# Gate and up as seven stacked half products from the fifth chunk on, with weight forms prepared in chunks 1 to 3

## Chip, core and metric

The kernel runs on one core of a Trainium2 chip. The metric is the device time of one execution in microseconds. The core has TensorE (PE, with weight loads shown apart as PEld), VectorE (DVE), ScalarE (ACT), GpSimd (POOL) and SyncE (SP), whose queue issues all DMA transfers here.

## What is computed

The reference normalises 8192 tokens of 448 channels, mixes them with a spectral block (a Fourier transform along the tokens, a two-layer block-diagonal network on the frequencies, the inverse transform), and then applies a gated feed-forward layer. All six modulation rows come from a small vector c.

```python
h = _layernorm(x) * (1 + ca) + sa
x = x + ga * _A_ref(h, A_w1, A_b1, A_w2, A_b2)      # rfft2, block MLP, irfft2
h = _layernorm(x) * (1 + cb) + sb
x = x + gb * ((_gelu(h @ w_gate) * (h @ w_up)) @ w_down)   # 448 -> 1792 -> 448
```

The change is in the last line's two first products, gate and up.

## The kernel before

Two stages follow each other. The spectral stage (up to about 383 us of the trace) works through frequency groups, in a list of steps; `at(i, ...)` puts side jobs into step i, among them the loading and splitting of the gate and up weights (`load_w`, `weights_hi`, `weights_lo`, lines 692 and 787 to 795, in steps 17 to 31). The feed-forward stage is a loop of 32 chunks `i` of 256 tokens (`CB` = 2 blocks of 128), and in it 14 ticks `k` (line 1272). Feature tile f of 128 is written as f = t + 7q, tile t from 0 to 6, half q 0 or 1, and k = 2t + q.

Every f16 product is done in a high and a low part: a value is scaled, its f16 rounding is the high part, the remainder the low part, and high x high, high x low and low x high are summed in PSUM. `gate_up` (line 1096) issues for a tick 20 matmuls of 256 columns (line 1087): gate and up, each with three full tiles of 128 of the 448 channels in three variants plus one half tile of 64 channels that carries two variants at once. The remaining low half tiles (64 rows) are issued for a pair of tiles together, two at a time on different halves of the array (lines 1112 to 1116). That makes 308 matmuls a chunk. `gate_up_out` (line 1120) takes gelu of the gate on ACT (1123), multiplies by up on DVE (1128) and forms four sums of the 2 x 2 blocks (two halves q, two token blocks) on POOL (1134 to 1137), in place in an eight-part tile x. `quantize` (1139) splits seven of the parts into f16 high on ACT (1145) and low on DVE (1146).

`down` (line 1158) multiplies them with seven weight forms (Strassen's scheme in Winograd's form: seven products of halves instead of eight): 7 products of 7 tiles of 3 matmuls with 224 columns (1153 to 1155), 147 a chunk. It runs for chunk i - 1 at tick k = 2 of chunk i, in one piece. ACT and DVE read the products, POOL finishes the rows (1190, 1167, 1168), and SP stores them (1197).

The same loop prepares chunk i + 2 at fixed ticks (`hooks`, line 1201): load of v, g and the tokens, `split_g` and `split_v` at k = 3 (high on ACT, low on POOL, line 107), `inverse` at k = 6 (987 to 989, six matmuls of 448 columns), `residual` (998, 999), statistics, `norm2` (1036, 1037), `pack_hi` and `pack_lo` at k = 13 (1042, 1049 to 1051), and at k = 0 of the next chunk four DMA transposes into `nt` (1057). The order of instructions on each engine is the order of the program text; an engine that waits holds up all that stands behind it. PSUM has eight banks: `pa` and `pb` for gate and up, `pc` and `pd` for the rest, two of each.

Of the kernel before, what the change touches and what calls it, by code (L numbers as in the profile page):

```python
# [10 lines left out]
F32 = mybir.dt.float32  # L11
# [26 lines left out]
NTT = len(PKO)  # L38
LAM = 0.01
# [6 lines left out]
def spectral_geglu(ctx, tc, x, w1, b1, w2, b2, wg, wu, wd, cvec, wmod, cf1, cs2, cmi, cgm, out):  # L46
# [10 lines left out]
    sd = dram.tile([NP, 128, 4, HC], F32, name="sd")  # L57

    cpool = ctx.enter_context(tc.tile_pool(name="cpool", bufs=1))
    psum = ctx.enter_context(tc.tile_pool(name="psum", bufs=2, space=bass.MemoryType.PSUM))  # L60
# [18 lines left out]
    sw = cpool.tile([128, 2], F32, name="sw")  # L79
    dg = cpool.tile([128, 1], F32, name="dg")  # L80
# [238 lines left out]
    with ExitStack() as bctx:  # L319
# [359 lines left out]
        def row_scales():  # L679

            GL.tensor_scalar(cb_r, cb_r, 1.0, None, op0=ALU.add)
            tiny.extend([free] * 2)
            for j, r in enumerate((cb_r, sb_r)):
                VL.tensor_reduce(rmax[:, j : j + 1], r, mybir.AxisListType.X, ALU.max, apply_absolute_value=True)
            bnd = cpool.tile([128, 1], F32, name="hb")
            VL.scalar_tensor_tensor(bnd, rmax[:, 0:1], 21.2, rmax[:, 1:2], op0=ALU.mult, op1=ALU.add)
            VL.tensor_scalar(bnd, bnd, 1.01, 1e-30, op0=ALU.mult, op1=ALU.add)
            pow2(sk, bnd)
            GL.tensor_scalar(sb_r, sb_r, sk, None, op0=ALU.mult)
            GL.tensor_scalar(cb_r, cb_r, sk, None, op0=ALU.mult)  # L690
# [48 lines left out]
        def scales1():  # L739

            ni = nrm.bitcast(I32)
            VL.tensor_scalar(ni, ni, 1, 0x7F800000, op0=ALU.logical_shift_right, op1=ALU.bitwise_and)
            VL.tensor_scalar(ni, ni, float(65 << 23), None, op0=ALU.add)
            mx = mpool.tile([128, 2], F32, name="mx")
            VL.tensor_reduce(mx, nrm, mybir.AxisListType.X, ALU.max)

            hb2 = mpool.tile([128, 1], F32, name="hb2")
            mx2 = mpool.tile([128, NFT], F32, name="mx2")
            first = [
                lambda: G.tensor_tensor(hb2, rmax[:, 0:1], rmax[:, 1:2], ALU.add),  # L750
                lambda: G.tensor_tensor(hb2, hb2, hb2, ALU.mult),
                lambda: G.tensor_scalar(hb2, hb2, 1.02 * D, 1e-30, op0=ALU.mult, op1=ALU.add),
            ]

            then = [
                lambda: G.tensor_tensor(mx2, nrm[:, 0], nrm[:, 1], ALU.mult),
                lambda: G.tensor_scalar(mx2, mx2, hb2, None, op0=ALU.mult),
            ]
            all_sum(mxa, mx, 2, first, then)
            pow2(sw, mxa)  # L760
            VL.tensor_tensor(sa_act, mx2[:, :NP], mx2[:, NP:], ALU.max)
# [24 lines left out]

        def weights_hi(pr, j):
            raw = raws[("w", pr, j)]
            fs = slice(pr * F + j * 256, pr * F + (j + 1) * 256)
            S.activation(wh[:, :, fs], raw, AF.Copy, scale=sw[:, pr : pr + 1])  # L790

        def weights_lo(pr, j):
            raw = raws.pop(("w", pr, j))
            fs = slice(pr * F + j * 256, pr * F + (j + 1) * 256)
            V.scalar_tensor_tensor(wl[:, :, fs], raw, sw[:, pr : pr + 1], wh[:, :, fs], op0=ALU.mult, op1=ALU.subtract)

# [52 lines left out]
        wpool = ctx.enter_context(tc.tile_pool(name="wpool", bufs=1))  # L852
        wh = wpool.tile([128, 4, 2 * F], F16, name="wh")
        wl = wpool.tile([128, 4, 2 * F], F16, name="wl")

# [3 lines left out]

        def x1_tile(i):  # L860

            pool, n = (cp, 2) if i % 3 else (ep, 1)
            return pool.tile([128, CB, D], F32, tag="x1", name="x1", bufs=n)
# [63 lines left out]

        fctx = ExitStack()
# [4 lines left out]
        for j in range(14):  # L933
            at(17 + j, "load", pre, fp, ("w", j % 2, j // 2), load_w, j % 2, j // 2)
            at(18 + j, "act", weights_hi, j % 2, j // 2)
            at(18 + j, "dve", weights_lo, j % 2, j // 2)
# [12 lines left out]
    with ExitStack() as cctx:  # L949
        cp = cctx.enter_context(tc.tile_pool(name="cp", bufs=1, side="right"))  # L950
        H = 128 * CB
        wds = wds + [cp.tile([128, 2, 7, HC], F16, name=f"wd{t}") for t in range(len(wds), NP)]
        nts, acts, pgu = {}, {}, {}

# [13 lines left out]
        def split_v(i, cs=slice(0, D)):  # L968
            n = nxt[i]
            if "vh" not in n:  # L970
                n["vh"] = cp.tile([128, CB, D], F32R, tag="vh", name="vh")
                n["vl"] = cp.tile([128, CB, D], F32R, tag="vl", name="vl")
            for b in each(i):
                split(n["vh"][:, b, cs], n["vl"][:, b, cs], n["v"][:, b, cs], el=G)
# [64 lines left out]
        def pack_hi(i):  # L1039
            pk = cp.tile([128, CB, PKW], F16, tag="pk", name="pk")  # L1040
            for b in each(i):
                S.copy(pk[:, b, 0:D], nxt[i]["n"][:, b])
            nxt[i]["pk"] = pk

        def pack_lo(i):
            n, pk = nxt[i]["n"], nxt[i]["pk"]
            for b in each(i):
                e = V if i == 0 else G
                e.tensor_tensor(pk[:, b, 448:512], n[:, b, 384:448], pk[:, b, 384:448], ALU.subtract)
                e.tensor_copy(pk[:, b, 512:576], pk[:, b, 384:448])  # L1050
                e.tensor_tensor(pk[:, b, 576:960], n[:, b, 0:384], pk[:, b, 0:384], ALU.subtract)
            nts[i] = cp.tile([128, NTT, H], F16, tag="nt", name="nt", bufs=2)

# [30 lines left out]
        def gu(i, t, q, pr, w, rows, tw, tn, start, stop):  # L1084

            f0 = pr * F + (t + NP * q) * 128
            T.matmul(  # L1087
                pgu[i, t, q][:, pr * H : (pr + 1) * H],
                w[rows, tw, f0 : f0 + 128],
# [6 lines left out]
        def gate_up(i, k):  # L1096
# [7 lines left out]
            seq = [(wh, j, j) for j in range(4)] + [(wh, j, j + 5) for j in range(3)] + [(wl, j, j) for j in range(3)]  # L1104
# [5 lines left out]
            elif q == 1:  # L1110

                for pr in range(2):
                    for u in range(2):
                        for qq in range(2):
                            it = divmod(i * NP + t + u, NP)
                            gu(*it, qq, pr, wl, halfs[qq], 3, 3 + qq, u == 1 and pr == 0, u == 0)
# [3 lines left out]
        def gate_up_out(i, t, q):  # L1120
# [6 lines left out]
            dst = x[:, 1:3] if q else x[:, 0::7]  # L1127
# [3 lines left out]
            if q:  # L1131
                e = V if (i, t) == (nch - 1, NP - 1) else G
                a11, a12, a22, s1, s2, s3, s4, a21 = (x[:, j] for j in range(8))
                e.tensor_tensor(s1, a21, a22, ALU.add)  # L1134
                e.tensor_tensor(s2, s1, a11, ALU.subtract)  # L1135
                e.tensor_tensor(s3, a11, a21, ALU.subtract)  # L1136
                e.tensor_tensor(s4, a12, s2, ALU.subtract)  # L1137
# [11 lines left out]
        def product(i, ps, ka, kb, ts=range(NP)):  # L1149
            ps = ps[:, :HC]  # L1150
            for t in ts:
                ac = acts[(i, t)]
                T.matmul(ps, ac[:, 0, ka], wds[t][:, 0, kb], start=t == 0, stop=False)  # L1153
                T.matmul(ps, ac[:, 0, ka], wds[t][:, 1, kb], start=False, stop=False)  # L1154
                T.matmul(ps, ac[:, 1, ka], wds[t][:, 0, kb], start=False, stop=t == NP - 1)  # L1155
            return ps

        def down(i):
            p1, p4, u2, u4 = (cp2.tile([128, HC], F32, tag=n, name=n) for n in ("p1", "p4", "u2", "u4"))
            o = cp2.tile([128, CB, D], F32, tag="o", name="o")  # L1160
# [11 lines left out]
            b1, b2 = bank("pd", "pdn"), bank("pc", "pdn")  # L1172

            product(i, b1, 0, 0, range(NP - 1))
            product(i, b2, 1, 1, range(NP - 1))
            S.copy(p1, product(i, b1, 0, 0, [NP - 1]))
            V.tensor_tensor(o11, product(i, b2, 1, 1, [NP - 1]), p1, ALU.add)
            if last:
                finish(0, 0, G)
            for fn, *args in second["down"] if i == 0 else []:  # L1180
                fn(2, *args)
            S.copy(p4, product(i, bank("pd", "pdn"), 2, 5))
            V.tensor_tensor(u2, product(i, bank("pd", "pdn"), 4, 6), p1, ALU.add)
            V.tensor_tensor(u4, product(i, bank("pd", "pdn"), 3, 3), u2, ALU.add)
            for fn, *args in second["down2"] if i == 0 else []:
                fn(2, *args)
            p7 = product(i, bank("pd", "pdn"), 5, 4)
# [3 lines left out]
            p3 = product(i, bank("pd", "pdn"), 6, 2)  # L1191
# [8 lines left out]

        hooks = {
            0: [(1, transposes_dma)],
# [8 lines left out]
            13: [(2, pack_hi), (2, pack_lo)],  # L1211
# [44 lines left out]
        cp2 = cctx.enter_context(tc.tile_pool(name="cp2", bufs=1))  # L1256
# [15 lines left out]
        for i in range(nch):  # L1272
            for k in range(NFT):
# [3 lines left out]
                if k % 2 == 1 and i + k > 1 and (i, k) != (nch - 1, NFT - 1):  # L1277
                    quantize(*((i, k // 2 - 1) if k > 1 else (i - 1, NP - 1)))
                if (i, k) == (nch - 1, NFT - 2):
                    quantize(i, NP - 2)  # L1280
# [3 lines left out]
                if k == 2 and i > 0:  # L1284
                    down(i - 1)
                    if i == 1:
                        transposes_dma(2, range(1, 2))
                for fn, *args in first.pop(i * NFT + k, []):
# [7 lines left out]
        quantize(nch - 1, NP - 1, (0, 3, 7))  # L1296
        down(nch - 1)
# [75 lines left out]
```

## Time and profile before

| what | value |
|---|---|
| median of 3 runs | 1938.26 us (1938.06 to 1939.17) |
| the profiled execution | 1940.48 us, its span 1938.7 us |
| granted TensorE clock, mean | 0.994 |
| instructions | 43005 |
| DMA moved | 163.79 MB, mean 84 GB/s |

A page or view of the profile covers the one profiled execution. An engine's busy time is the time in which one of its instructions was executing; a matmul's time is modelled from start to drain, so matmuls that follow at 109 ns are each shown with 273 ns. In a group's row stand line, engine, operation, tiles written and read, shape and count, then busy time in us, mean ns of one, then idle time of the engine before them and who ended it. In a windows row stand the window, its length, the busy time (and count) of each engine, the granted clock, the DMA share and GB/s.

### The profile page before, as it was taken

Reading aid. Unit: us, or ns where it says so; the run is one execution under the profiler, and the core shown is the slowest. Engines: PE = TensorE matmul, PEld = TensorE weight load, DVE = VectorE, ACT = ScalarE, POOL = GpSimd, SP = SyncE. Lnnn points to the kernel's source line nnn. Section 1 sums busy time; section 2 is a strip of 40 time slices with the busy share of each in tenths; the row PEclk is TensorE's granted clock in tenths of the full one; section 3 lists DMA queues with packets and bytes.
Section 4 is the critical chain, followed back from the end, with each engine's and each line's share of the span. In section 5 each row is a group of like instructions: output and inputs, shape, how many; then the busy total and the mean of one; then the engine's idle time right before and its main releaser. Section 6 shows DMA issues by size and latency. Waiting matters only on the chain.

```text
span 1938.7 us, 43005 instructions
## 1 busy us (share of the span) xinstructions
PE 1903.1 (98%) x17620; PEld 1694.9 (87%) x17620; DVE 1109.8 (57%) x2352; ACT 788.3 (41%) x1338; POOL 1159.4 (60%) x1466
## 2 busy tenths in 40 slices
PE   7899999899999999999999999999999999999999
PEld 3599999778888888888888888888888888888898
DVE  8677788786555555555555555555555555555533
ACT  5677888553333333333333333333333333333322
POOL 3157655256666666666666666666666666666644
PEclk9899999999999999999999999999999999999999
DMA  9999777641111111111111112111111111111000
GB/s 346 314 286 257 203 188 197 171 140 49 45 43 45 43 41 45 45 41 46 41 46 43 42 44 44 43 43 44 43 44 43 43 43 43 43 43 43 21 11 20
DMA packets 157981, 163.79 MB, mean 84 GB/s; under 512 B 77908, under 2 KB 136152, under 8 KB 157784
## 3 DMA queue, kind: packets, MB, share of 16 engines
q1 hardware_dynamic: 157784, 161.05, 28.7%
q8 instruction: 138, 2.26, 0.5%
q14 instruction: 59, 0.48, 0.1%
HBM read 97.44 MB, written 47.25 MB: 75 GB/s over the span
## 4 chain that ended last, share of the span: by engine, by line
PE 86%; DVE 4%; issue 3%; ACT 3%; DMA 2%; POOL 2%; SPq 1%; ACTq 0%; POOLq 0%; DVEq 0%
PE pgu L1087 53%; PE pdn L1155 8%; PE pdn L1154 8%; PE pdn L1153 8%; PE ps L202 2%; DVE y L463 2%; PE pi L989 1%; PE pi L988 1%; PE pi L987 1%; POOL yl L107 1%; DMA raw<-in_B_w_up 1%; DVE st L163 0%; ACT th L105 0%; PE ps L368 0%; PE ps L370 0%
## 5 line engine op out<-in xcount | busy, mean ns | idle before, releaser
L1087 PE MATMUL pgu<-nt,wh 128*128 128x256 f16 x6272 | 834.3, 273 | 2.7 <-DVE x L1128 2.6
L1087 PEld LDWEIGHTS <-wh 128*128 128x128 f16 x6272 | 602.7, 98 | 101.5 <-issue 33.9
L1123 ACT ACTIVATE gel<-pgu,dg 128x256 f32<-128x256 f32 x448 | 200.3, 473 | 792.3 <-PE pgu L1087 756.2
L1087 PE MATMUL pgu<-nt,wl 128*128 128x256 f16 (+1 forms) x3584 | 501.3, 272 | 0.4 <-DVE x L1128 0.4
L1155 PE MATMUL pdn<-wd,ac 128*128 128x224 f16 x1568 | 406.1, 259 | 0.2 <-DVE ac L1146 0.2
L1153 PE MATMUL pdn<-wd,ac 128*128 128x224 f16 x1568 | 406.1, 259 | 0.0
L1154 PE MATMUL pdn<-wd,ac 128*128 128x224 f16 x1568 | 406.1, 259 | 0.0
L1134 POOL TENSOR_TENSOR x<-x 128x128 f32<-128x128 f32 x223 | 239.9, 1076 | 260.3 <-DVE x L1128 228.1
L1146 DVE SCALAR_TENSOR_TENSOR ac<-x,sa_act,ac 128x896 f16<-128x896 f32 (+1 forms) x225 | 308.9, 1373 | 83.3 <-ACT ac L1145 83.3
L1087 PEld LDWEIGHTS <-wl 128*128 128x128 f16 (+1 forms) x3584 | 297.9, 97 | 57.5 <-issue 24.3
L1128 DVE TENSOR_TENSOR x<-pgu,gel 128x256 f32<-128x256 f32 x448 | 179.6, 418 | 276.2 <-ACT gel L1123 275.6
L1145 ACT ACTIVATE ac<-x,sa_act 128x896 f16<-128x896 f32 (+1 forms) x225 | 232.9, 1035 | 49.0 <-POOL x L1137 47.0
L1190 POOL TENSOR_TENSOR o<-u,p 128x224 f32<-128x224 f32 x32 | 21.0, 657 | 291.8 <-DVE u L1189 291.8
L1135 POOL TENSOR_TENSOR x<-x 128x128 f32<-128x128 f32 x223 | 157.5, 706 | 17.5
L1155 PEld LDWEIGHTS <-ac 128*128 128x128 f16 x1568 | 153.4, 98 | 0.5 <-DVE ac L1146 0.5
L1154 PEld LDWEIGHTS <-ac 128*128 128x128 f16 x1568 | 153.4, 98 | 0.4
L1153 PEld LDWEIGHTS <-ac 128*128 128x128 f16 x1568 | 153.4, 98 | 0.4
L107 POOL TENSOR_TENSOR yl<-y,yh 128x448 fp32r<-128x448 f32 x63 | 78.9, 1252 | 75.6 <-ACT yh L105 64.4
L463 DVE SCALAR_TENSOR_TENSOR y<-pm,t 64x224 f32<-64x224 f32 x256 | 99.5, 389 | 41.3 <-ACT t L455 37.4
L1136 POOL TENSOR_TENSOR x<-x 128x128 f32<-128x128 f32 x223 | 113.7, 510 | 0.0
L1137 POOL TENSOR_TENSOR x<-x 128x128 f32<-128x128 f32 x223 | 110.7, 497 | 0.0
L107 POOL TENSOR_TENSOR tl<-tr,th 128x896 f16<-128x896 f32 x30 | 57.3, 1909 | 68.3 <-DMA td<-xt 36.8
(281 smaller groups left out, 2727.7 us busy)
## 6 DMA issues: line engine op xcount, KB each, us to landing
tr<-td SPq DMA_DIRECT2D x64, 224.0 KB, 4.2
vd<-us SPq DMA_DIRECT2D x64, 224.0 KB, 3.5
xx<-in_A_x SPq DMA_DIRECT2D x32, 448.0 KB, 3.2
v<-vd SPq DMA_DIRECT2D x63, 224.0 KB, 2.9
out<-x SPq DMA_DIRECT2D x31, 448.0 KB, 2.7
xt<-in_A_x SPq DMA_DIRECT2D x15, 896.0 KB, 15.3
td<-xt SPq DMA_DIRECT2D x48, 224.0 KB, 4.4
s<-cs SPq DMA_DIRECT2D x20, 256.0 KB, 4.5
```

What stands on the lines that cost most here:

```text
L107: (el or V).tensor_tensor(lo, src, h, ALU.subtract)
L463: V.scalar_tensor_tensor(y[ri * 64 : ri * 64 + 64, gi], pv[si, ri], LAM, tv[si, ri], op0=ALU.add, op1=ALU.min)
L1087: T.matmul(pgu[i, t, q][:, pr * H : (pr + 1) * H], w[rows, tw, f0 : f0 + 128], nts[i][rows, tn, :], start=start, stop=stop, skip_group_che ...
L1123: S.activation(gl, ps[:, :H], AF.Gelu_apprx_tanh, scale=dg)
L1128: V.tensor_tensor(dst, ps[:, H : 2 * H].rearrange("p (b c) -> p b c", b=2), gl.rearrange("p (b c) -> p b c", b=2), ALU.mult)
L1134: e.tensor_tensor(s1, a21, a22, ALU.add)
L1135: e.tensor_tensor(s2, s1, a11, ALU.subtract)
L1145: S.activation(ac[:, 0, k], x[:, k], AF.Copy, scale=sc)
L1146: V.scalar_tensor_tensor(ac[:, 1, k], x[:, k], sc, ac[:, 0, k], op0=ALU.mult, op1=ALU.subtract)
L1153: T.matmul(ps, ac[:, 0, ka], wds[t][:, 0, kb], start=t == 0, stop=False)
L1154: T.matmul(ps, ac[:, 0, ka], wds[t][:, 1, kb], start=False, stop=False)
L1155: T.matmul(ps, ac[:, 1, ka], wds[t][:, 0, kb], start=False, stop=t == NP - 1)
```

## The change

Chunks 0 to 3 (`NSTD` = 4) keep the plain scheme. From chunk 4 on gate and up are computed with seven products as `down` already is: the halves are the two halves q of the features, the two token blocks, and the two halves of 192 channels; the last 64 channels are stacked beside the halves so that tiles of 128 rows are full. One (chunk, tile) is a "period" u = 7i + t. Its matmuls have 128 columns, alternate between gate and up (two banks of one of three PSUM sets), and come in stages a, b, c, d. Partial results are copied inside PSUM (`seed`), out of it (`copy_b`) and joined (`joins`), so a period's work is spread over four: stage_a of u, stage_d of u - 2, stage_c of u - 1, stage_b of u. `down` of chunk i - 1 and the new `winverse` of chunk i + 2 run after the period of tile 2 (`phase`).

The weights' seven forms are made during chunks 1 to 3 (`prep`): loaded, summed on POOL, split on ACT and DVE, and stored to DRAM (`wk`). SBUF holds four slots, each for the forms of one tile; up to chunk 3 the plain weights lie in them. Tiles are visited forward and backward in turn, so that three slots a chunk are loaded again from `wk` (`load_part`, in two parts). The token forms are made on DVE (`token_sums`), ACT (`wpack_hi`) and POOL (`wpack_lo`), and five DMA transposes bring 25 tiles into `nt` (before four bring 8 tiles of 256 columns). The low part of v now lies in v itself. The weights of the spectral stage are loaded by six DMA starts each where it was three, and the scale factor uses another power of two. The core of the diff:

```diff
+NSTD = 4
+WPARTS = ((0, 4), (4, 7))
+    wk = [[dram.tile([128, 2, 2, 2, b - a, 128], F16, name=f"wk{t}{a}") for a, b in WPARTS] for t in range(NP)]
...
+        def load_w2(pool, pr, j):
+            raw = raw_tile(pool).rearrange("p k c -> p (k c)").rearrange("p (e k f) -> p e k f", e=2, k=4)
+            for e in range(2):
+                wsrc = (wg, wu)[pr][:, (2 * j + e) * 128 : (2 * j + e + 1) * 128]
+                dma(raw[:, e, 0:3], wsrc[0:384].rearrange("(t p) f -> p t f", p=128))
+                for rows in rows2:
+                    dma(raw[rows, e, 3], wsrc[384:448])
+            return raw
...
         def weights_hi(pr, j):
-            S.activation(wh[:, :, fs], raw, AF.Copy, scale=sw[:, pr : pr + 1])
+            for w, r in weight_cuts(pr, j):
+                S.activation(w[:, :, 0], r, AF.Copy, scale=sw[:, pr : pr + 1])
...
+        wslot = [wpool.tile([128, 2, 2, 14, 128], F16, name=f"wk{n}") for n in range(4)]
...
-        def down(i):
+        def down(i, banks, mid=lambda n: None):
...
+        def load_part(u, part):
+            a, b = WPARTS[part]
+            dst = wslot[slot_of[u]].rearrange("p r l (g f) x -> p (r l g) f x", g=2)
+            dma(dst[:, :, a:b], wk[torder[u]][part].rearrange("p r l g f x -> p (r l g) f x"))
+        def after(u, part):
+            if u in refill:
+                pending.append((refill[u], part))
...
+        def wpack_lo(i, ks, e=G):
+            for k in ks:
+                for src, hi, los in pieces(i, k):
+                    for a, b, lo in los:
+                        e.tensor_tensor(lo, src[..., a:b], hi[..., a:b], ALU.subtract)
+        def wtransposes(i, gs, w=5):
+            for g in gs:
+                nc.sync.dma_start(
+                    nts[i][:, w * g : w * g + w, :], pkt[:, 128 * w * g : 128 * w * (g + 1)], transpose=True
+                )
...
+        def mm(u, reg, f, x, start=False):
+            ps2, slot, nt = sets[u % 3], wslot[slot_of[u]], nts[u // NP]
+            if f in (A11, S1, S2):
+                terms = [(0, f, x), (0, f, x + 2), (1, f, x), (0, 7 + f, x + 1), (1, 7 + f, x + 1)]
+            else:
+                terms = [(l, f + 7 * g, x + g + 2 * m) for g in range(2) for l, m in ((0, 0), (0, 1), (1, 0))]
+            for j, (hl, wt, xt) in enumerate(terms):
+                for pr in range(2):
+                    T.matmul(
+                        ps2[:, pr, reg * 128 : reg * 128 + 128],
+                        slot[:, pr, hl, wt, :],
+                        nt[:, xt, :],
...
+        def stage_a(u):
+            mm(u, RY, A11, B11, start=True)
+            mm(u, RV, S1, T1)
+            mm(u, RX, A12, B21)
+        def stage_b(u):
+            mm(u, RY, S2, T2)
+        def stage_c(u):
+            mm(u, RV, S3, T3)
+            mm(u, RY, S4, B22)
+        def stage_d(u):
+            mm(u, RV, A22, T4)
+        def copy_b(u):
+            S.copy(sbs[u], sets[u % 3][:, :, 0:256])
+        def seed(u):
+            S.copy(p[:, :, 0:128], p[:, :, 128:256])
+        def joins(u):
+            V.tensor_tensor(c[:, :, 1:3, :], p[:, :, 0:256]..., b[:, :, 0:128]..., ALU.add)
+            V.tensor_tensor(c[:, :, 0, :], p[:, :, 256:384], b[:, :, 128:256], ALU.add)
...
+        def period(u):
+            on(u, stage_a)
+            on(u - 1, seed)
+            for fn, *args in held:
+                fn(*args)
+            held.clear()
+            on(u - 2, joins)
+            on(u - 2, gel3)
+            on(u - 4, quant_lo)
+            on(u - 2, mult3)
+            on(u, copy_b)
+            on(u - 2, stage_d)
+            on(u - 2, lambda v: after(v, 1))
+            on(u - 2, gel1)
+            on(u - 2, mult1)
+            on(u - 2, lambda v: sums(xs[v], G))
+            on(u - 3, quant_hi)
+            on(u - 1, stage_c)
+            on(u, stage_b)
+            on(u, lambda v: after(v, 0))
...
+        def phase(i):
+            pf = sets[(u + 1) % 3]
+            on(u - 3, quant_lo)
+            if j < nch:
+                winverse(j, pf)
+                residual(j)
+            down(i - 1, down_banks(pf), mid)
+        extra = {
+            1: [(2, split_v), (2, split_g), (1, wtransposes, [0])],
+            2: [(1, wtransposes, range(1, 5))],
+            3: [(2, token_sums, 0), (2, wpack_hi, [0, 1]), (2, wpack_lo, [0, 1])],
+            4: [(2, token_sums, 1), (2, wpack_hi, [2]), (2, wpack_lo, [2])],
+            5: [(2, wpack_hi, [3]), (2, wpack_lo, [3]), (3, load_g)],
+            6: [(2, wpack_hi, [4]), (2, wpack_lo, [4]), (3, load_v)],
+        }
...
+                (0, load_forms),
+                (1, form_sums, 0),
+                (1, forms_hi, 0),
+                (2, forms_lo, 0),
+                (2, forms_hi, 1),
+                (2, forms_lo, 1),
+                (3, form_sums, 1),
+                (3, store_forms, 0),
+                (4, forms_hi, 2),
+                (4, forms_hi, 3),
+                (4, forms_lo, 2),
+                (5, forms_lo, 3),
+                (5, store_forms, 1),
+            ):
+                prep.setdefault(NFT + 6 * n + s, []).append((fn, n, *args))
...
+        for u in range(U0, NT_ + 1):
+            period(u)
+            flush()
+            if k == LA:
+                phase(i)
```

`gel3`, `mult3` and the first three quarters of a tile's result (384 columns) come before stage_d, `gel1` and `mult1` (128 columns) after it; `quant_hi` and `quant_lo` do what `quantize` did. `flush` issues the pending loads of weight forms.

## Prediction before the run

> **What bounds the kernel now.** I read the page first, then the busy time by stage, then the groups by line and shape, and last the timeline of single matmuls.
>
> ```profile
> PE 1903.1 (98%) x17620; PEld 1694.9 (87%) x17620; DVE 1109.8 (57%) x2352; ACT 788.3 (41%) x1338; POOL 1159.4 (60%) x1466
> ...
> PE   7899999899999999999999999999999999999999
> ```
>
> TensorE (PE) is busy in every slice and the other engines are not. The next view holds two chunks, all instructions first and then those of L1087 (gate and up) alone:
>
> ```profile
> 812.96:909.44 96.48, 96.48 (x925) 86.34 (x923) 50.33 (x101) 31.42 (x53) 62.25 (x81) 1.00 0.17 44
> ```
>
> ```profile
> 812.96:909.44 96.48, 66.35 (x619) 56.22 (x617) 1.00 0.17 44
> ```
>
> PE has no idle time there at full clock. The code gives 308 gate and up matmuls a chunk, and 2 x 308 = 616 is the 619 of the row with its edges, so a chunk takes 48.24 us. How that divides, from the timeline of PE:
>
> ```profile
> 814.78 0.93 PE L1087 MATMUL pgu<-nt,wh 128*128 128x256 f16 x7
> 815.55 0.49 PE L1087 MATMUL pgu<-nt,wl 128*128 128x256 f16 x3
> 815.88 0.93 PE L1087 MATMUL pgu<-nt,wh 128*128 128x256 f16 x7
> ...
> 819.15 0.26 PE L1153 MATMUL pdn<-wd,ac 128*128 128x224 f16 x1
> ...
> 821.93 0.26 PE L1155 MATMUL pdn<-wd,ac 128*128 128x224 f16 x1
> ...
> 842.54 0.45 PE L987 MATMUL pi<-vh,gh 128*128 128x448 f32 x1
> ...
> 843.66 0.36 PE L989 MATMUL pi<-vl,gh 128*128 128x448 f32 x1
> ```
>
> Ten matmuls of 256 columns start in 815.88 - 814.78 = 1.10 us, 109 ns each. The down matmuls (30 rows from 819.15 to 821.93, 29 steps) come every 96 ns, so the 147 of a chunk take 14.1 us. The six inverse matmuls take 1.3 us. Gate and up keep 48.24 - 14.1 - 1.3 = **32.8 us a chunk**. Anything that gains must shorten that.
>
> **The change part by part. TensorE in chunks 4 to 31.** For one feature tile pair (a "period" of the new loop) stage_a issues 10 + 10 + 12 matmuls, stage_b 10, stage_c 24, stage_d 12: 78 of 128 columns, 546 a chunk, each with a weight load of its own. Columns fall from 308 x 256, less the 14 pairs of half matmuls that run side by side, to 546 x 128, but weight loads rise from 308 to 546. So everything hangs on how fast a load and a 128-column matmul follow each other. The trace has this shape in the spectral stage and in chunk 0:
>
> ```profile
> 117.49 0.22 PE L369 MATMUL ps<-s,th 128*112 128x128 f16 x1
> ...
> 118.72 0.22 PE L370 MATMUL ps<-s,tl 128*112 128x128 f16 x1
> ```
>
> ```profile
> 383.24 0.61 PE L1069 MATMUL ptr<-ident,pk 128*128 128x128 f16 x8
> ```
>
> Of the first stretch these are the first and the last of 23 rows, 22 steps in 1.23 us: 55.9 ns. The eight with full 128x128 weights end 0.61 us after the first began; less one duration of 0.22, seven steps, 55.7 ns. I take 55.9: 546 x 55.9 = 30.5 us, **2.3 us a chunk less, 28 chunks: -64 us**.
>
> The Trainium skill ("TensorE: Matmul & The Clock Gate", section "Back-to-back issue gap") speaks against this: in a stream of load and matmul pairs it gives about 81 ns at 128 columns, which would make an estimated 44.2 us a chunk and the kernel some 320 us slower. This trace disagrees, in short runs only (55.9 ns over 23); a run of 78 is not in it, so the rule stays as the pace of a rival below.
>
> **The other engines inside a period of 78 x 55.9 = 4.36 us.** Times of one instruction, chunks 7 to 15:
>
> ```profile
> L1145 ACT ACTIVATE ac<-x,sa_act 128x896 f16<-128x896 f32 x59 | 61.3, 1038 | 11.7 <-POOL x L1137 11.6
> L1123 ACT ACTIVATE gel<-pgu,dg 128x256 f32<-128x256 f32 x118 | 52.8, 473 | 210.9 <-PE pgu L1087 201.1 <-DVE rcy L118 6.8 <-DVE x L1128 3.0
> ...
> L1176 ACT COPY p<-pdn 128x224 f32<-128x224 f32 x8 | 2.8, 346 | 29.1 <-PE pdn L1155 29.1
> ```
>
> ```profile
> L1146 DVE SCALAR_TENSOR_TENSOR ac<-x,sa_act,ac 128x896 f16<-128x896 f32 x59 | 82.0, 1389 | 20.7 <-ACT ac L1145 20.7
> L1128 DVE TENSOR_TENSOR x<-pgu,gel 128x256 f32<-128x256 f32 x118 | 47.2, 417 | 73.1 <-ACT gel L1123 72.9
> ```
>
> ```profile
> L1134 POOL TENSOR_TENSOR x<-x 128x128 f32<-128x128 f32 x59 | 65.9, 1117 | 59.1 <-DVE x L1128 59.1
> L1135 POOL TENSOR_TENSOR x<-x 128x128 f32<-128x128 f32 x58 | 39.7, 684 | 4.5
> L1136 POOL TENSOR_TENSOR x<-x 128x128 f32<-128x128 f32 x58 | 29.4, 507 | 0.0
> L1137 POOL TENSOR_TENSOR x<-x 128x128 f32<-128x128 f32 x58 | 27.9, 480 | 0.0
> L999 POOL TENSOR_TENSOR x<-x,xx 128x448 f32<-128x448 f32 x18 | 20.0, 1131 | 0.0
> L107 POOL TENSOR_TENSOR vl<-v,vh 128x896 fp32r<-128x896 f32 x9 | 18.8, 2092 | 0.0
> ...
> L1051 POOL TENSOR_TENSOR pk<-n,pk 128x768 f16<-128x768 f32 x8 | 13.2, 1646 | 0.0
> L107 POOL TENSOR_TENSOR gl<-g,gh 128x256 fp32r<-128x256 f32 x8 | 5.8, 722 | 0.0
> ```
>
> ACT: 224 columns cost 346 ns and 896 cost 1038, so about 1.03 ns a column above 0.12. seed (256 columns) 0.38, copy_b (512) 0.65, the two gelus (384 and 128, with L1123's 0.09 more) 0.6 and 0.35, quant_hi 1.04, a piece of wpack_hi 0.3 to 0.8: 3.3 to 3.8 us. DVE: joins (512 and 256 columns) 0.7 + 0.42, quant_lo 1.39, mult3 0.55, mult1 0.3: 3.4. POOL: the four sums 1.12 + 0.68 + 0.51 + 0.48 = 2.79, and wpack_lo's 1600 columns at 1646/768 = 2.1 ns with their overheads, 4.4 us a chunk in four periods: 2.8 to 4.2. All fit, and their waits are covered: b waits for copy_b behind 2.0 us of d and c, c waits for seed behind 2.5 us of a and d, d waits for the joins behind a's 1.8. I charge these **nothing**; the cover ends if an engine needs more than 4.36 us (first rival).
>
> One wait is not covered. split_v and split_g stand on POOL behind the sums of k=1, in the last period before the new winverse. In k=1 stage_d ends 2.45 us in, gel1 at 3.1 and mult1 at 3.5, or at 3.8 where ACT or DVE runs late; the sums end 2.79 later, 1.9 to 2.3 us into k=2, and 2.09 + 0.72 more end at 4.75 to 5.1. Winverse's second matmul wants gl at 4.36 + 0.2. I take the middle, **0.4 us a chunk, +11 us**. Bounds are 0 (POOL's spans are rough and it may be ahead of this) and 2.0 us (the wait and a late refill together). In down nothing else is late: its last tile's quant_lo ends some 1.5 us after the period, and 36 products lie ahead of it, 3.4 us.
>
> **Weight refills.** Three slots a chunk, 5.5 MB, are new on SP's queue. There they stand behind the out store, which waits for POOL's finish (four operations of 1.13, till 4.4 us after down), and four transposes:
>
> ```profile
> 867.02 6.40 SPq L1057 DMA_TRANSPOSE nt<-pk  x4
> ```
>
> ```profile
> xx<-in_A_x SPq DMA_DIRECT2D x32, 448.0 KB, 3.2
> ```
>
> The transposes hold SP for 6.4 us or, with five tiles for four, 8. The second half of the second refill (0.79 MB; 3.2 us by the xx row, twice that at worst) is issued near 11 to 12.5 and lands at 14 to 19 us. stage_c wants it 3 x 4.36 + 2.45 = 15.5 us after down. I take it as just in time: 0.
>
> **Chunks 0 to 3 keep their matmuls,** but chunks 1 to 3 also make the forms.
>
> ```profile
> 425.40:571.20 145.80, 145.80 (x1384) 129.99 (x1382) 82.72 (x174) 47.07 (x80) 93.15 (x118) 1.00 0.18 50
> ```
>
> The columns after the length are PE, loads, DVE, ACT, POOL. Each of seven tiles adds on POOL four sums of 384 columns (0.97 each by L999) and a copy, some 4.9 us. ACT and DVE add 1792 columns, twice their 896-column rows with ten starts: about 3.3 and 3.6. POOL goes to 93.2 + 34 = 127 of 145.8, DVE to 108, ACT to 70. Outside down a chunk has 34 us of PE and POOL would have 31 + 11.5 = 42.6 us of work, so it is 8.4 late when the last tile's sums stand in its queue. The down product needs that tile 10.4 us after its gelu, and its own chain (2.8 + 1.04 + 1.39) takes 5.2: 3.2 us late a chunk, **+10 us** in three chunks. Bounds: 0 and, if ACT also waits for each form load, 25.
>
> **The rest.** The switch at chunk 4 empties the pipeline: the last gelu and product (0.9) and the first copy_b (0.9) are uncovered, and at the end the last tile has its chain of joins, gelus, sums and quant (some 7 us by the times above) behind 63 down matmuls (6.0), an estimated 1 us uncovered: **+3 us**, between 1 and 6. The 14 weight loads of the spectral stage become 84 starts instead of 42, and some ACT and DVE instructions split in two; PE's nines in slices 4 to 8 hide that: 0, at most 3 without that cover.
>
> Sum: -64 + 11 + 10 + 3 = **-40 us**. The profiled execution took 1940.48 us for a span of 1938.7, the median is 1938.26; that span with the 1.8 us around it is 2.2 above the median. I subtract from the median: **1898 us**.
>
> **The rivals.**
>
> *POOL becomes the bound (slower).* A POOL operation that meets a long DVE operation on SBUF is stretched:
>
> ```profile
> 1865.40 1.36 POOL L1135 TENSOR_TENSOR x<-x 128x128 f32<-128x128 f32 x1
> 1866.39 0.42 DVE L1128 TENSOR_TENSOR x<-pgu,gel 128x256 f32<-128x256 f32 x1
> 1866.72 0.45 POOL L1136 TENSOR_TENSOR x<-x 128x128 f32<-128x128 f32 x1
> ```
>
> That is 0.9 us. A tile now has two such DVE operations (quant_lo and mult3) where it had one. Sums with two stretched operations take 4 x 0.45 + 2 x 0.9 = 3.6 us, with wpack_lo's piece 4.7; in four or five periods a chunk PE then waits 0.35 to 0.45, 1.8 us a chunk: 1898 + 50 = **1948**. It decides from 40/28/7 = 0.20 us a period upward. Against it: POOL can pay back in down's 14 us. 11%.
>
> *Refills late.* With landings between 15.5 and 19 us, in the middle 17.2, stage_c waits 1.7 us a chunk: 1898 + 48 = **1946**. For it: the queue is in order and the margin small. Against: the transfers average only 44 GB/s now (last column of the windows). 6%.
>
> *The loads set the pace:* the matmuls do not do what their columns say.
>
> ```profile
> L1087 PEld LDWEIGHTS <-wh 128*128 128x128 f16 x6272 | 602.7, 98 | 101.5 <-issue 33.9
> ```
>
> A load lasts 98 ns. If in a long run loads followed one another, 546 x 98 = 53.5 us, 20.7 more than now: **about 2520**. It decides from 32.8/546 = 60 ns. Against it stand the 55.9 ns, at which loads must overlap. By the skill's 81 ns it would be an estimated 2260. 4%.
>
> *Forecast, 79%:* PE-bound with few waits; its own range runs from no wait at all (1938 - 64 + 1 = 1875) to each cost at about twice its value, 1922.
>
> **How the numbers follow.** Range 1874 to 1950: from the forecast without waits up to the POOL and refill cases; left out are the slow loads, 4%, and the far ends of the other three. About 0.2% (4 us) is what a measurement can tell here. Faster: 75 of the forecast's 79, 1 of POOL's 11 and 1 of the refills' 6, 77%. Same: 3 + 2 + 1 = 6%. Slower: 1 + 8 + 4 + 4 = 17%.
>
> **What would show it.** Matmuls of 128 columns 56 ns apart inside a stage, and a chunk of 46.5 us or less (30.5 + 14.1 + 1.3 + 0.4) between two copies of p1. A wait of PE for POOL's gl at winverse of about 0.4 us. In chunks 1 to 3 PE waiting at down for the last ac, some 3 us. If steps inside a stage exceed 60 ns, or PE waits in most periods for sb, RV's seed or the joins, the prediction is wrong; if PE waits at stage_c for DMA, the refill case holds.

## The result and the profile after

The changed kernel takes 2149.39 us (2148.29 to 2151.15) where the kernel before takes 1938.16: a ratio of **1.109** (95% interval 1.1071 to 1.111). The forecast was 1898 us in a range of 1874 to 1950; the time is 211 us above the kernel before, beyond the rivals at 1946 and 1948 us and short of the one at 2520, and none of these mechanisms turned out to be the cause. From the page of the kernel after, the busy times and two rows of the 40 slices, PE and the granted clock:

```profile
PE 1919.0 (89%) x24284; PEld 1817.2 (85%) x24284; DVE 1467.5 (68%) x2957; ACT 1022.5 (48%) x1915; POOL 1177.7 (55%) x1643
...
PE   7899999886673899999999999999989999999998
...
PEclk9999999997876899999999999999999999999999
```

TensorE is idle for 11% of the span, and from the tenth to the fourteenth slice (483 to 751 us, chunks 1 to 4) it is both idle and at a lower granted clock. Where the time went is read from the copy of down's first product (p1), one a chunk, in the view of one source line. Four copies cover the stretch of the preparation, 26 copies a stretch of the new loop; first the kernel before, then after:

```profile
L1176 ACT COPY p<-pdn x4: 346/346/346, 437.1 to 582.1; 128x224 f32<-128x224 f32 x4
```

```profile
L1176 ACT COPY p<-pdn x26: 346/346/346, 630.1 to 1836.8; 128x224 f32<-128x224 f32 x26
```

```profile
L1218 ACT COPY p<-pdn x4: 324/346/346, 437.4 to 718.8; 128x224 f32<-128x224 f32 x4
```

```profile
L1218 ACT COPY p<-pdn x26: 346/346/347, 771.9 to 2046.9; 128x224 f32<-128x224 f32 x26
```

The preparation stretch grew from 145.0 to 281.4 us: **+136**. A chunk of the new loop takes (2046.9 - 771.9)/25 = 51.0 us where the plain chunk took 48.3: **+2.7**, some 76 us over 28 chunks, where 2 us less had been forecast. The two are the whole loss. Of the 279 us of the windows row of this stretch (last section), PE is busy for 178: it stands still for some 101, and what it does takes some 33 longer than before, about 6 of them because the copy stands later in the chunks of the new loop, the rest at a granted clock of 0.79 in the mean.

Who waited, in the preparation stretch of the kernel after, first PE, then ACT (total, times, longest):

```profile
PE pgu L1118 <- DVE x L1159: 41.1, 8, 8.0
PE set L1350 <- DVE x L1159: 29.0, 1, 29.0
PE pdn L1191 <- ACT ac L1178: 11.7, 2, 7.7
```

```profile
ACT ws L1557 <- DMA wk<-ws: 72.8, 7, 14.6
ACT ws L1557 <- DMA wr<-in_B_w_up: 51.1, 6, 14.4
```

PE waits for products and for the quantised ac, but those stand behind ACT's gelu, and ACT stands for 124 us in the weight forms: 72.8 for the store of a tile's first part (`ws` has one buffer, and the second part is written into it) and 51.1 for the next tile's load (`wr` has one buffer, and its load starts when the last low part has been read). PE's one wait of 29.0 us is the switch: ahead of the last gelu stand ACT's last wait for a load (14.4 us, until 671.58) and its last wait for a store (11.5 us, until 690.04). In the new loop, 25 chunks:

```profile
PE set L1350 <- ACT sb L1378: 68.8, 25, 3.9
PE set L1460 <- DVE x L1410: 7.9, 23, 0.3
```

```profile
ACT pk L1321 <- DMA nt<-pk: 114.7, 25, 5.7
```

PE waits for copy_b once a chunk, 2.75 us in the mean, and ACT for a transpose, 4.6 us in the mean. One such place in ACT's timeline and SP's shows why:

```profile
1040.93 0.35 ACT L1321 CAST pk<-n 128x192 f16<-128x192 f32 x1
1046.93 0.40 ACT L1321 CAST pk<-n 128x256 f16<-128x256 f32 x1 [5.65 <-DMA nt<-pk]
1047.24 0.61 ACT L1399 ACTIVATE gl<-c,dg 128x384 f32<-128x384 f32 x1
1047.76 0.56 ACT L1378 COPY sb<-set 128x512 f32<-128x512 f32 x1
```

```profile
1040.68 0.38 SPq L1241 DMA_DIRECT2D out<-x  x1
1041.11 6.49 SPq L1333 DMA_TRANSPOSE nt<-pk  x4
```

The token forms of the next chunk are packed into the one `pkt`. The four transposes that read it stand behind the out store, which is issued at 1040.68; they end near 1047, and wpack_hi's second piece waits for them with gel3 and copy_b behind it in ACT's queue. The wait costs once more, in three windows of the same place (PEclk is the third value from the end):

```profile
1040.60:1047.20 6.60, 3.92 (x68) 3.68 (x66) 2.90 (x5) 0.89 (x3) 3.56 (x8) 1.00 0.91 147
1047.20:1054.00 6.80, 5.62 (x54) 5.62 (x54) 4.59 (x9) 4.20 (x9) 4.36 (x9) 0.50 0.85 245
1054.00:1060.00 6.00, 6.00 (x110) 6.00 (x109) 3.41 (x7) 4.48 (x8) 3.42 (x7) 1.00 0.56 191
```

PE waits 3.82 us, from 1044.56 to 1048.38, and from 1047.2 on the granted clock is 0.50 for 6.8 us. The Trainium skill ("TensorE: Matmul & The Clock Gate", "What's actually happening") has the clock halved after an idle window of about 3.4 us. This trace agrees only in part. Half a clock comes with all six waits of the 25 chunks that are longer than 3.4 us, in four of them 2.1 to 2.6 us after the wait began. It also comes with 13 of the 19 shorter waits, among them five of the eleven that last about 2.1 us. One of those five and the window behind it:

```profile
1453.80:1455.90 2.10, 0.00 (x1) 0.00 (x0) 0.49 (x1) 1.44 (x4) 0.67 (x1) 1.00 0.56 113
1456.80:1460.20 3.40, 3.40 (x36) 3.40 (x34) 3.35 (x6) 1.79 (x5) 1.86 (x4) 0.50 0.84 244
```

### The profile page after: what moved, and what is told of

Its sections match the earlier page's. It is cut to its first block, busy times and chain, and to the rows that moved or that the text cites. A ratio compares the mean times of both kernels' runs of the same rounds, so it can differ in the third digit from the quotient of the medians.

```text
span 2146.5 us, 58651 instructions
## 1 busy us (share of the span) xinstructions
PE 1919.0 (89%) x24284; PEld 1817.2 (85%) x24284; DVE 1467.5 (68%) x2957; ACT 1022.5 (48%) x1915; POOL 1177.7 (55%) x1643
## 4 chain that ended last, share of the span: by engine, by line
PE 52%; DVE 14%; DMA 11%; POOL 9%; SPq 5%; ACT 4%; issue 4%; ACTq 0%; POOLq 0%; DVEq 0%
PE set L1350 25%; PE pdn L1193 4%; DMA nt<-pk 4%; PE pdn L1191 4%; PE pdn L1192 4%; DVE ac L1425 3%; POOL x L1206 3%; POOL o L1205 3%; PE set L1191 2%; PE set L1192 2%; PE set L1193 2%; SPq L1333 2%; DVE ws L1561 1%; DVE y L471 1%; PE ps L210 1%
## 5 line engine op out<-in xcount | busy, mean ns | idle before, releaser
L1350 PE MATMUL set<-nt,wk 128*128 128x128 f16 x15288 | 911.1, 224 | 111.4 <-ACT sb L1378 76.8
L1350 PEld LDWEIGHTS <-wk 128*128 128x128 f16 x15288 | 901.1, 101 | 119.2 <-issue 117.1
L1191 PE MATMUL pdn<-wd,ac 128*128 128x224 f16 x1162 | 303.1, 261 | 12.3 <-ACT ac L1178 11.7
L1193 PE MATMUL pdn<-wd,ac 128*128 128x224 f16 x1162 | 302.7, 260 | 3.3 <-DVE ac L1179 2.1
L1192 PE MATMUL pdn<-wd,ac 128*128 128x224 f16 x1162 | 302.8, 261 | 0.0
L1425 DVE SCALAR_TENSOR_TENSOR ac<-x,sa_act,ac 128x896 f16<-128x896 f32 x196 | 277.0, 1414 | 1.3 <-ACT ac L1415 1.3
L1167 POOL TENSOR_TENSOR x<-x 128x128 f32<-128x128 f32 x223 | 120.3, 539 | 251.4 <-DVE x L1403 142.4
L1403 DVE TENSOR_TENSOR x<-c,gl 128x384 f32<-128x384 f32 x196 | 179.0, 913 | 109.8 <-ACT gl L1399 109.7
L1415 ACT ACTIVATE ac<-x,sa_act 128x896 f16<-128x896 f32 x196 | 202.3, 1032 | 0.6 <-DVE x L1170 0.4
L1118 PE MATMUL pgu<-nt,wk 128*128 128x256 f16 (+1 forms) x1232 | 154.5, 295 | 44.0 <-DVE x L1159 43.9
L1118 PEld LDWEIGHTS <-wk 128*128 128x128 f16 (+1 forms) x1232 | 121.8, 105 | 76.6 <-issue 54.7
L1387 DVE TENSOR_TENSOR c<-set,sb 128x512 f32<-128x512 f32 x196 | 134.6, 687 | 74.2 <-PE set L1350 74.2
L1168 POOL TENSOR_TENSOR x<-x 128x128 f32<-128x128 f32 x223 | 126.6, 568 | 17.5
```

The lines of the kernel that those rows point to most:

```text
L1118: T.matmul(pgu[i, t, q][:, pr * H : (pr + 1) * H], ws[rows, n, w, tw], nts[i][rows, tn, :], start=start, stop=stop, skip_group_check=True,)
L1191: T.matmul(ps, ac[:, 0, ka], w[:, 0, kb], start=n == 0, stop=False)
L1192: T.matmul(ps, ac[:, 0, ka], w[:, 1, kb], start=False, stop=False)
L1193: T.matmul(ps, ac[:, 1, ka], w[:, 0, kb], start=False, stop=n == NP - 1)
L1350: T.matmul(ps2[:, pr, reg * 128 : reg * 128 + 128], slot[:, pr, hl, wt, :], nt[:, xt, :], start=start and j == 0, stop=j == len(terms) - 1 ...
L1387: V.tensor_tensor(c[:, :, 1:3, :], p[:, :, 0:256].rearrange("p g (r c) -> p g r c", r=2), b[:, :, 0:128].rearrange("p g (o c) -> p g o c", ...
```

## The experiments

The theory: the loop itself keeps its pace, and two single buffers whose release is a DMA round trip stop ACT. The rivals: dense 128-column matmuls hold the clock or the pace down by themselves; the preparation's own work (POOL's sums, as forecast) costs the time. All kernels below start from the changed one. "Stretch" is from the first p1 copy to the one that ends the preparation and the switch, "chunk" is that of the new loop.

**All transposes at tile 1, ahead of the out store.**

```diff
-            1: [(2, split_v), (2, split_g), (1, wtransposes, [0])],
-            2: [(1, wtransposes, range(1, 5))],
+            1: [(2, split_v), (2, split_g), (1, wtransposes, range(5))],
+            2: [],
```

> All five transposes of a chunk stand in SP's queue at tile 1, ahead of the out store, instead of four behind it. Theory (token forms' single buffer: ACT waits 5.7 us a chunk for the transposes and PE 2.75 us for copy_b behind it, then the clock halves): that ACT wait goes, the PE wait for sb goes, the half-clock windows after chunk 4 go, a chunk takes about 46.8 us instead of 51.0, the whole 28 x 4.2 = 118 us less, near 2030 us. Rival (loads of 128-column matmuls or their power hold the clock down in any case): the half-clock windows stay every chunk, a chunk stays above 49 us and the time above 2095 us. The preparation in chunks 1 to 3 stays as long as it is (about 280 us between the first and fourth p1 copy) by both.

Measured: 2030.96 us, ratio to the kernel before 1.0476 (1.0461 to 1.0492). The p1 copies and PE's only wait of the new loop, then one chunk's gate and up in the timeline of PE:

```profile
L1218 ACT COPY p<-pdn x26: 346/347/347, 766.8 to 1930.1; 128x224 f32<-128x224 f32 x26
```

```profile
PE set L1460 <- DVE x L1410: 8.2, 24, 0.4
```

```profile
1010.02 30.84 PE L1350 MATMUL set<-nt,wk 128*128 128x128 f16 x546
```

A chunk takes 46.5 us at full clock, the wait for sb is gone, and 546 matmuls run without a break: (30.84 - 0.22)/545 = 56.2 ns each. The first rival falls. Of the 4.5 us a chunk that came back 2.75 were PE's wait. The rest, 1.7, fits the half clock: in the 25 chunks of the changed kernel its 19 windows of 3.4 or 6.8 us last 82 us, which at half speed cost 41, or 1.6 a chunk.

**The late transposes ahead of down, still at tile 2.** The four transposes are issued just before `phase(i)`.

> The kernel after the change with one move: the four late transposes of a chunk are issued ahead of down and its out store, at the same tile 2. Theory (they were late because the out store in front of them waits for POOL's last rows): as with all five at tile 1, a chunk of 46.6 us and about 2031 us. Rival (6.5 us of transposes are too long wherever they stand between tile 2 and tile 4): a chunk above 48.5 us and the time above 2080.

Measured, in one run: 2029.10 us, a chunk of (1929.1 - 765.9)/25 = 46.5. So it was the place behind the out store, which waits for POOL's last rows; the transposes' own 6.5 us fit.

**Two store buffers.** x gives up its third buffer to make the room.

```diff
-            return cp.tile([128, 8, 128], F32, tag="x8", name="x8", bufs=3)
+            return cp.tile([128, 8, 128], F32, tag="x8", name="x8", bufs=2)
...
-                raws[("s", t)] = cp2.tile([128, 2, 4, 4 - part // 2, 128], F16, tag="ws", name="ws")
+                raws[("s", t)] = cp2.tile([128, 2, 4, 4 - part // 2, 128], F16, tag=f"ws{part}", name="ws")
```

> The two parts of a tile's weight forms get a buffer each (the eight-part tile x gives up its third buffer for that). Theory (ACT waits in order for the store of the first part, 72.8 us in all, and PE runs out behind it): those waits go, the waits for the form load (51 us) stay or grow by a little, and the time falls by about 60 us to near 2090 us. Rival (POOL is overloaded by the form sums, as the prediction had it): the time between the first and fourth p1 copy stays near 280 us and the time within 15 us of 2149.

Measured: 2117.74 us, ratio 1.0925 (1.0907 to 1.0944), stretch 250.1. ACT's waits for stores are gone, but only 32 us come back, half of what was expected and short of both ranges: ACT still waits for loads (45.9 us after 51.1) and now also for POOL's sums.

```profile
ACT ws L1557 <- DMA wr<-in_B_w_up: 45.9, 6, 13.9
ACT ws L1557 <- POOL wr L1531: 23.8, 5, 6.9
```

**Two store buffers and an early load.** The load moves to four ticks ahead of its use, the parts to ticks 2 to 5 of a tile's six.

```diff
-                (0, load_forms),
-                (1, form_sums, 0),
-                (1, forms_hi, 0),
-                (2, forms_lo, 0),
+                (-2, load_forms),
+                (2, form_sums, 0),
+                (2, forms_hi, 0),
+                (3, forms_lo, 0),
```

> As the run with two buffers, and the load of the next tile is issued as soon as the last low part is made, four ticks ahead of its first use instead of one. Theory: ACT's waits for load and store both fall under 20 us in all, the stretch from the first to the fourth p1 copy falls from 281 to 150 to 165 us (145 before), the time by 115 to 130 to about 2025 us. Rival (POOL overload): the stretch stays above 200 us, the time above 2070.

Measured: 2079.00 us, ratio 1.0725 (1.0709 to 1.0741), stretch 210.6 instead of the 150 to 165 expected. The load wait fell to 14.5 us, the store wait is gone, and 66 us more than the plain 145 are still there, as the rival had it. Two buffers, the early load and the later places of the parts together take away half of the preparation's loss. Of the 66, PE stands still for 46 (it is busy for 164.9 of the 210.6 us), 6 are the later place of p1, and 14 are the same work at a lower clock, 0.89 in the mean.

**Both: early transposes, two stores, early load.**

> Both changes: early transposes, and the preparation with two buffers and an early load. Theory: the gains add, 118 + 120, so about 1910 us, and a chunk of about 46.8 us against 48.2 before, so 1.5% faster than the kernel before. Rival (clock held down by dense 128-column matmuls): above 1980 us.

Measured: 1960.89 us, ratio 1.0113 (1.0098 to 1.0128), a stretch of 211.2. The gains add, 118 + 70, but the expected 1910 is missed by the same 50 us as in the run before.

**Two x buffers alone, with early transposes.**

> Early transposes with two buffers of the eight-part tile x instead of three, a control for the runs that took its third buffer away. Theory: a chunk of 46.8 us instead of 46.6 as in the run with both changes, and chunks 0 to 3 longer by less than 5 us: 2035 to 2040. Rival: the smaller x also holds up the plain chunks, by 20 us or more, and hides part of what two store buffers give: 2050 or above.

Measured, in one run: 2034.54 us, a chunk of (1935.4 - 768.3)/25 = 46.7, a stretch of 282.4. The smaller x costs about 4 us in all and does not explain the missing 50.

**Forms for one tile only, early transposes.** All slots are loaded from tile 0's forms.

> Early transposes, and forms are made for tile 0 alone; all slots are loaded from that tile's forms, so gate and up use tile 0's weights for all tiles and the output is not the reference's. Theory (each tile's preparation costs about 19 us of waiting, 8.5 for its load and 10.4 for its store): six tiles less take 6 x 19 = 114 us away, near 1917 us. Rival (the loss in the first chunks comes from the switch to the new loop and its token forms): at most 40 us less, above 1990.

Measured, in one run: 1916.54 us, as expected, and a stretch of 167.2. Six tiles less are worth 114 us, 19 a tile. That is the sum of round trips and work; it does not part them. It does show what else is lost: 22 us over the plain 145 are left. Some 6 of these only move p1 from after three ticks (6.9 us) to after three tiles (13.1 us) in its chunk; about 3 of them come back at the end (from the last p1 copy but one to the end of the span 52.3 us, 55.3 in the kernel before). PE stands still for 10.5 us, 5.8 of them at the switch. The others are at the inverse transform in chunk 1, where POOL's low parts of g and v stand behind 2.8 us of form sums and the copy for the store:

```profile
PE pi L1019 <- POOL gl L115: 2.9, 1, 2.9
PE pi L1020 <- POOL v L115: 1.6, 1, 1.6
```

ACT waits 11.3 us for the one store here, and no wait of PE for the gelu behind it follows. The remaining 5.5 us come with the lower clock, 0.95 in the mean.

**Ten ticks a tile, single buffers, early transposes.** `NSTD` = 6, the parts at ticks 3, 4, 5 and 9 of ten.

> Early transposes, and the forms are made in chunks 1 to 5 instead of 1 to 3, ten ticks a tile instead of six, with the single buffers as they were: four ticks lie between each load or store and the instruction that needs it. Theory (prep loses time only because load and store round trips of about 9 us each stand inside six ticks): chunks 1 to 5 take about 48.5 to 50 us each as before, the 26 later chunks 46.6 instead of 48.2, so 1938 - 26 x 1.6 + some 10 = about 1907 us, faster than the kernel before. Rival (the work of the preparation itself, POOL's sums above all, costs PE time): the first five chunks lose 40 us or more and the time is 1940 or above.

Measured: 1956.52 us, ratio 1.009 (1.0075 to 1.0104), where the theory gave 1907: a miss, on the side of the rival. ACT's waits for loads fell to 5.8 us and for stores to nothing, and still five chunks and the switch take 742.2 - 437.3 = 304.9 us, 63 more than five plain chunks. PE stands still for 39 of them. Its longest waits there:

```profile
PE pgu L1118 <- DVE x L1159: 13.5, 10, 2.7
PE set L1350 <- DVE x L1159: 6.4, 1, 6.4
PE set L1350 <- ACT sb L1378: 6.3, 1, 6.3
PE pi L1020 <- POOL v L115: 4.7, 3, 2.4
```

With the round trips away the work of the parts is left: DVE's timeline ahead of such a wait shows form parts, normalisation and then the product that PE needs.

```profile
646.35 0.88 DVE L1067 SCALAR_TENSOR_TENSOR n<-x,cmv,cb_r 128x448 f32<-128x448 f32 x1
647.26 0.76 DVE L1068 SCALAR_TENSOR_TENSOR n<-n,rcy,sb_r 128x448 f32<-128x448 f32 x1
647.95 2.54 DVE L1561 SCALAR_TENSOR_TENSOR ws<-wr,sww,ws 128x384 f16<-128x384 f32 x3
650.42 1.41 DVE L1067 SCALAR_TENSOR_TENSOR n<-x,cmv,cb_r 128x448 f32<-128x448 f32 x1
651.86 0.69 DVE L1068 SCALAR_TENSOR_TENSOR n<-n,rcy,sb_r 128x448 f32<-128x448 f32 x1
652.46 0.75 DVE L1159 TENSOR_TENSOR x<-pgu,gel 128x256 f32<-128x256 f32 x2
```

**One or two parts a tick, ten ticks, two stores.**

> Ten ticks a tile in chunks 1 to 5 as before, but with two store buffers (x has two) so that the parts can follow one another at one high and one low part a tick. Theory (bunching): of the 63 us lost in the first five chunks some 40 come back: 26 chunks gain 1.4 each, 36, less 8 for the switch and 15 for the parts: about 1926 us. Rival (work as such): the loss stays above 50 us, 1950 or above.

Measured: 1957.41 us, ratio 1.0098 (1.0084 to 1.0112), five chunks and the switch in 735.5 - 436.4 = 299.1 us. Spreading the parts evenly gained 6 of the 63 us, about what the smaller x costs in the 26 later chunks, and the time did not move, as the rival had it: bunching alone is not the cause.

**One tile a chunk in chunks 1 to 7, single buffers.** `NSTD` = 8: first half at ticks 4 to 6, second half at ticks 0 and 1 of the next chunk, 24 chunks in the new loop.

> Early transposes, and the forms are made one tile a chunk in chunks 1 to 7, with the single buffers, and no tick holds more than two parts: sums, high and low parts at ticks 4 to 6, the second half at ticks 0 and 1 where down gives the other engines 14 us. The new loop then runs 24 chunks instead of 28. Theory (what the run with ten ticks a tile lost, 63 us, is parts bunched in one tick that hold up the gelu, the product and the split in front of PE, not load or store waits): chunks 1 to 7 cost under 2 us each above 48.2, the switch about 8, and 24 chunks gain 1.6 each: 1939 - 38 + 8 + 7 = about 1915 us, faster than the kernel before by over 1%. Rival (the parts' 18 us of DVE, POOL and ACT work a tile cost PE about as much wherever they stand): 40 us or more are lost again, 1945 or above.

Measured: 1938.74 us, ratio 0.9993 (0.9984 to 1.0002): no difference from the kernel before, between theory and rival. From p1 of chunk 0 to that of chunk 6 the trace has 746.1 - 437.2 = 308.9 us, 289.6 for plain chunks: 3.2 us a tile. One of these waits, DVE's timeline:

```profile
466.73 0.41 DVE L1159 TENSOR_TENSOR x<-pgu,gel 128x256 f32<-128x256 f32 x1
469.50 0.63 DVE L1038 BATCH_NORM_STATS2 cst<-x 128x6 f32<-128x448 f32 x1 [2.37 <-POOL x L1030]
470.59 0.63 DVE L1038 BATCH_NORM_STATS2 cst<-x 128x6 f32<-128x448 f32 x1 [0.46 <-POOL x L1030]
471.13 0.30 DVE L1041 BATCH_NORM_AGGREGATE cmv<-cst 128x2 f32<-128x6 f32 x2
471.35 0.39 DVE L1159 TENSOR_TENSOR x<-pgu,gel 128x256 f32<-128x256 f32 x1
```

POOL, late by the form sums at tick 6, brings residual late; DVE's statistics wait for it and the product stands behind them. The prediction had POOL late by these sums too, but at another place (the last tile's sums ahead of down). That both give 3.2 us is chance: the prediction had 2.3 tiles in a chunk, this run has one. The switch costs 813.6 - 746.1 = 67.5 us against 48.3 plus the 6 by which p1 moves.

**One tile a chunk, around down.** As before, but sums, first and second half stand ahead of and inside `down`, with two store buffers.

> Early transposes; one tile's forms a chunk in chunks 1 to 7, all of them around down at tick 2, where PE has 14 us of products and DVE, ACT and POOL little to do: first half ahead of down's readers, second half between them, with two store buffers (x has two). Theory (the parts cost PE time only where they stand in an engine's queue ahead of a gelu, product or split that PE needs soon): the chunks 1 to 7 cost under 1 us each above 48.2, the switch under 10, 24 later chunks gain 1.4 each: 1939 - 34 + 10 + 5 = about 1920 us, faster than the kernel before. Rival (about 18 us of engine work a tile slows PE wherever it stands): as the run with a tile a chunk, 1935 to 1945.

Measured: 1933.33 us, ratio 0.9971 (0.9959 to 0.9982), **0.3% faster than the kernel before** and the best version found; expected were 1920, and by the time alone the rival, from 1935 up, was nearer. Six chunks take 746.2 - 439.7 = 306.5 us, of which the first has 8.6 too much (down's reader u2 behind normalisation and parts, 4.1 us), the others 1.7 each, mainly PE's wait for the p1 copy, which now stands behind high parts:

```profile
PE pdn L1191 <- ACT p L1218: 10.1, 7, 3.4
PE pdn L1191 <- DVE u L1227: 4.1, 1, 4.1
```

So the work as such is not the whole price either: at this place it costs 1.7 us a tile beyond the first, in the places of the changed kernel, with its round trips, 19.

## Why the prediction was wrong, point by point

- **The pace of the matmuls** was right: 56.2 ns in a run of 546 for the 55.9 taken from 23. By the Trainium skill's 81 ns that run would have lasted an estimated 44.2 us; it lasted 30.8, so for this stream the measurement decides. The third rival (the loads set the pace) falls, and with it the only case whose price was as large as the result.
- **The sum of a chunk** was right where nothing waits: 30.5 + 14.1 + 1.3 + 0.4 = 46.3 us forecast, 46.5 measured with early transposes. In the 0.4 the size is luck: it stood for POOL's gl, but PE waits there 0.34 us a chunk for DVE's `mult1` (L1410), which by the code reads the bank that winverse writes next.
- **The step that failed in the loop** is "I charge these nothing". ACT, DVE and POOL do fit into a period, and refills and POOL were no bound, but the cover was worked out for the waits inside a period alone. The part on refills had the right order on SP's queue (out store, POOL's finish, then transposes until about 11 us after down) and used it only for the refills. The same transposes also read the single `pkt` that wpack_hi writes in the second period after down. By the prediction's own numbers the transposes end their issue near 11 us; wpack_hi wants to write at 4.36 + 0.8. Measured: ACT waits 4.6 us a chunk in the mean (5.7 at most), PE 2.75, and half a clock adds 1.7 more: 4.5 us a chunk, 118 in all.
- **The step that failed in chunks 1 to 3** is "+10 us ... Bounds: 0 and, if ACT also waits for each form load, 25". It counted work and took 3.2 us a chunk for POOL. The measured stretch is 136 longer, 19 us a tile. Two buffers are refilled through DMA inside six ticks: the load wait was put into a bound and sized at 25 us in all (it is 51), and the store wait (73) was not seen at all: `forms_hi` of the second part writes the buffer that `store_forms` of the first still reads. The work was mis-sized too. The parts were taken as two 896-column rows a tile, 3.6 us on DVE and 3.3 on ACT; on DVE they took 55.0 us, 7.9 a tile, on ACT 37.6, 5.4 a tile:

```profile
L1561 DVE SCALAR_TENSOR_TENSOR ws<-wr,sww,ws 128x384 f16<-128x384 f32 x35 | 28.8, 838 | 73.7 <-ACT ws L1557 73.7
L1561 DVE SCALAR_TENSOR_TENSOR ws<-wr,sww,ws 128x128 f16<-128x128 f32 x14 | 11.5, 820 | 0.0
L1561 DVE SCALAR_TENSOR_TENSOR ws<-wf,sww,ws 128x384 f16<-128x384 f32 x14 | 10.0, 712 | 0.0
L1561 DVE SCALAR_TENSOR_TENSOR ws<-wr,sww,ws 128x256 f16<-128x256 f32 x7 | 4.7, 671 | 0.0
```

With this, the fullest engine of a plain-length preparation is not POOL at 127 of 145.8 us but DVE, at 82.7 + 55.0 = 138 instead of the forecast's 108. POOL's 4.9 us a tile were right.
- **The switch** was put at 3 us; 7 to 13 are seen beyond the move of p1 (61.4 us in the last run, 67.5 in the one before it, less 48.3 and 6.2), and of these 6.2 only some 3 come back at the end. In these two runs PE waits 3.3 and 7.0 us for the last product, which stands behind normalisation (in the second also behind form parts) in DVE's queue, and 3.5 and 1.9 us for the first copy_b.
- **The rivals:** POOL as the bound of a period did not show (no wait of PE on POOL in the new loop). Late refills did not show either: from 780 to 2050 us none of PE's waits is for `wk`, and one of 1.9 us follows at 2073.
- **What stays open:** how the 46 us for which PE stands still in the run with two store buffers and an early load divide between late POOL sums and DVE's parts ahead of products. PE's waits name DVE's product for 27.8 of them, 12.6 of these at the switch, but not what made DVE late. The runs suggest that the place decides (19, then 3.2, then 1.7 us a tile), but each changed several things at once.

## What to carry to other kernels

For each buffer that is not doubled, ask who must be done before its next writer may start, and when that writer stands in an in-order queue, what stands behind it: a DMA that reads the buffer, an issue queue that holds this DMA back, and the engine whose output that queue waits for belong to one chain. A timing that was worked out for one consumer (here the refills) has to be held against every other (here the next writer). Side work is best put where the bound engine has a long stretch that needs little of the others, and its price is read from who waits behind it, not from busy shares.

## What the runs showed of the hardware

- Weight loads of 98 ns overlap fully with 128-column matmuls: 546 in a row at 56.2 ns, one load each, at a granted clock of 1.00.
- A wait of PE can cost a second time through a half clock of 3.4 or 6.8 us. In the new loop of the changed kernel this came with all six waits of over 3.4 us and with five of the eleven of about 2.1; in the run with a tile a chunk it came with two of the six waits of 1.4 to 2.1 us in chunks 1 to 7. In the preparation stretch the mean granted clock was 0.79:

```profile
440.00:719.00 279.00, 177.78 (x1481) 147.03 (x1479) 130.70 (x237) 83.17 (x160) 142.21 (x170) 0.79 0.50 127
```

- The refills were cheap: in the new loop DMA moved 154 GB/s (last column), 44 in the two chunks shown of before, and PE waited for none of them in this window:

```profile
771.90:2046.90 1275.00, 1195.97 (x17471) 1178.22 (x17470) 903.49 (x1723) 569.54 (x1098) 758.34 (x1121) 0.97 0.55 154
```
